# Infini-attention and GEGLU in one kernel: attention output kept transposed up to the output projection

## The chip, the cores and the metric

The kernel runs on one core of one Trainium2 chip. The metric is device time in microseconds (us) of one execution. The engines are TensorE (PE in the profile, PEld for its weight loads), VectorE (DVE), ScalarE (ACT), GpSimd (POOL) and SyncE (SP), which here issues every DMA.

## What is computed

One pre-norm transformer layer in fp32 on 2048 rows of 512. The attention has 32 heads of 16 columns and four segments of 512 rows; beside the softmax within a segment, each head reads a running memory M, z of the segments before:

```python
for s in range(N):                                   # 4 segments of L = 512 rows
    logits = einsum("bhqd,bhkd->bhqk", qs, ks) * scale + mask      # causal
    a_dot = einsum("bhqk,bhkd->bhqd", softmax(logits), vs)
    num = einsum("bhld,bhde->bhle", phi(qs), M)
    den = einsum("bhld,bhd->bhl", phi(qs), z)[..., None] + 1e-6
    outs.append(g * num / den + (1.0 - g) * a_dot)   # g = sigmoid(beta), one per head
    M = M + einsum("bhld,bhle->bhde", phi(ks), vs)
    z = z + einsum("bhld->bhd", phi(ks))
h = x + concat_heads(outs) @ wo
out = h + (gelu(n @ w_gate) * (n @ w_up)) @ w_down   # n = layernorm(h), 1376 hidden columns
```

## The kernel before, in words

**Units.** The attention works through 16 units: a chunk c of 8 heads (128 columns) in a segment s, listed in `UNITS`, segments 0 and 1 for all chunks first, then 2 and 3. A unit has two halves of four heads, numbered Q. For each unit `qkv` (L582) projects q and k (L536) and, for two chunks at once, v (L565); splits them into a high and a low part; and scatters those with DMAs into the stacked operands `stq` and `stk` (L609, L615, with a mask row L620). `pass_a` (L687) multiplies them a first time (L701) and DVE takes each row's maximum (L711), which a small transpose (L734) and a DMA (L739) put into `stq`. `pass_b` (L742) multiplies them again the other way round (L756), ScalarE takes the exponential (L760), GpSimd masks the diagonal blocks (L764), and TensorE forms P V with four heads side by side (L785, four column tiles of 32). Its result, `pv`, is transposed: for each of four heads 32 rows (16 of values, the 17th the sum of the probabilities), with the 512 queries along the columns.

**After P V.** ScalarE copies `pv` to `pvs` (L804). TensorE transposes it in four blocks (L808), so that queries stand on partitions; DVE inverts the sums (L820), multiplies them by 1 - g (L821) and scales the values (L824); GpSimd adds the memory's part (L829); a DMA stores the half's 64 columns to `o_dram` (L835).

**The memory.** `mem` (L652), for segments after the first, multiplies phi(q) as the stationary operand by the state `mb` (8 heads by 17 columns) in four matmuls (L664), two to a PSUM bank, queries again on partitions. DVE adds 1e-6, inverts, multiplies by g and scales (L671 to L681). The state is formed in `qkv`: a product (L640), masked to each head's own block on DVE (L643), added to the one before on GpSimd (L648).

**The projection.** `wo_seg` (L843) loads 128 rows of `o_dram` (L850) and of x (L851), transposes the former in four blocks (L855), splits them into high and low parts on ScalarE and DVE (L506, L507), multiplies by `wo` (L862), adds x (L866) and stores h (L868). `ln2` and the feed-forward part follow (L1031, L1092), in two passes over the halves of the rows; rows of segments 2 and 3 are read again for the second pass (L1138).

**The order.** Nothing is in program order. Each operation is given to `Sched` (L114) with an engine, an assumed duration, a priority number and the values that it reads and writes. `run` (L149) lists the operations one engine at a time: it takes the lowest priority number among those that could start within 0.059 us of the earliest. Tiles come from pools (`Pool_`, L33) when an operation is placed and return when the last user is done. The planner assumes 0.58 us for a DMA's issue and 2.2 us until it has landed. Matmuls in four column tiles are a mode of their own ("c"); a change of mode is priced at 0.1 us and held off by another 0.1. On the chip each engine and the SP queue go through their lists strictly in order and wait where an input is late.

## Time and profile before

| what | value |
|---|---|
| median of 3 runs | 850.38 us (849.77 to 851.44) |
| the profiled execution | 850.29 us |
| its span in the trace | 848.2 us |
| instructions | 15681 |
| DMA packets | 64179, 82.90 MB, mean 98 GB/s |

The page gives for each engine the time that it was busy, the chain of work that ended last (followed back from the last instruction) and the costliest groups of instructions by line. A group's row has the tile written and read, shapes, count, busy time and mean of one, and the idle time ahead of them with what ended it. A row of the timeline has the start in us from the span's start, the duration, the engine, the line and how many instructions of a kind are merged. Matmuls are pipelined, so that the durations of neighbours overlap.

### The profile page before, as it was taken

The page shows a single profiled execution, that of the slowest core. Times are in us where ns is not written, and L with a number is a line of the kernel's source. Part 1 is how long each engine was busy: PE and PEld are TensorE (multiplying, and loading weights), DVE is VectorE, ACT ScalarE, POOL GpSimd, SP SyncE. Part 2 cuts the span into 40 slices and gives each one's busy share as a digit, 9 for nine tenths or more (in the row PEclk, how much of TensorE's full clock was granted, in tenths as well). Part 3 has the DMA queues.
Part 4 walks back from the last instruction along what each step waited for, and adds up shares of the span by engine and source line. Part 5 has one row for each costly group of instructions (what it writes and reads, how often), then busy time and mean ns, then how long its engine had stood idle before and what let it go on. Part 6 is the DMA issues. An engine that isn't in the chain of part 4 may idle for free.

```text
span 848.2 us, 15681 instructions
## 1 busy us (share of the span) xinstructions
PE 825.0 (97%) x4924; PEld 656.3 (77%) x4924; DVE 621.8 (73%) x1963; ACT 511.7 (60%) x966; POOL 458.7 (54%) x791
## 2 busy tenths in 40 slices
...
GB/s 248 120 119 96 96 74 69 108 103 96 85 121 122 89 85 97 48 121 90 107 122 122 126 230 143 122 72 63 63 51 62 119 158 38 50 63 62 51 1 100
DMA packets 64179, 82.90 MB, mean 98 GB/s; under 512 B 25056, under 2 KB 27040, under 8 KB 64096
## 3 DMA queue, kind: packets, MB, share of 16 engines
...
q14 instruction: 44, 0.36, 0.2%
...
## 4 chain that ended last, share of the span: by engine, by line
PE 92%; DVE 4%; ACT 2%; issue 1%; DMA 1%; SPq 0%; POOL 0%; ACTq 0%; DVEq 0%; POOLq 0%
PE bank L1031 24%; PE bank L1092 14%; PE bank L536 10%; PE bank L701 9%; PE bank L756 9%; PE bank L785 8%; PE bank L862 5%; PE bank L565 4%; PE bank L497 2%; PE bank L808 2%; PE bank L664 1%; PE bank L640 1%; PE bank L632 1%; PE bank L855 1%; ACT pt L760 1%
## 5 line engine op out<-in xcount | busy, mean ns | idle before, releaser
L711 DVE CUSTOM_DVE_ANT_0 junk<-bank,amask 128x256 f32<-128x256 f32 (+3 forms) x512 | 231.0, 486 | 54.1 <-PE bank L701 49.8
L764 POOL TENSOR_SCALAR_AFFINE_SELECT pt<-pt 128x128 f32<-128x128 f32 (+1 forms) x448 | 131.8, 314 | 202.5 <-ACT pt L760 192.1
L760 ACT ACTIVATE pt<-bank 128x512 f32<-128x512 f32 x320 | 177.8, 602 | 63.0 <-PE bank L756 50.4
L701 PE MATMUL bank<-stk,stq 128*128 128x512 f32 (+2 forms) x384 | 130.5, 386 | 0.9 <-DVE nm L711 0.5
L756 PE MATMUL bank<-stq,stk 128*128 128x384 f32 (+3 forms) x512 | 119.8, 325 | 1.3 <-ACT pt L760 0.8
L536 PE MATMUL bank<-xt,w 128*128 128x512 f32 x384 | 109.2, 397 | 0.0
L756 PEld LDWEIGHTS bank<-stq,stk 128*128 128x128 f32 x512 | 85.8, 189 | 15.4 <-ACT pt L760 6.2
L1097 DVE TENSOR_TENSOR pt<-pt,bank 128x512 f32<-128x512 f32 x96 | 64.9, 685 | 28.7 <-PE bank L1092 28.3
L701 PEld LDWEIGHTS bank<-stk,stq 128*128 128x128 f32 x384 | 66.8, 189 | 19.5 <-issue 9.3
L536 PEld LDWEIGHTS bank<-xt,w 128*128 128x128 f32 x384 | 70.0, 189 | 10.9
L785 PE MATMUL bank<-pt,vaug 128*32 128x512 f32 (+3 forms) x1024 | 76.0, 436 | 0.0
L785 PEld LDWEIGHTS bank<-pt,vaug 128*32 128x32 f32 x1024 | 28.4, 109 | 39.9 <-issue 31.8
L1001 POOL TENSOR_TENSOR w<-raw,w 128x512 fp32r<-128x512 f32 (+2 forms) x36 | 42.4, 1180 | 25.4 <-ACT w L999 24.1
L394 POOL TENSOR_TENSOR w<-raw,w 128x512 fp32r<-128x512 f32 (+1 forms) x26 | 34.1, 1312 | 40.6 <-ACT w L389 24.0
L1031 PE MATMUL bank<-xt,stk 128*128 128x512 f32 (+1 forms) x189 | 53.0, 394 | 0.3 <-ACT pq L1038 0.3
L565 PE MATMUL bank<-wv,xt 128*128 128x256 f32 x384 | 52.7, 284 | 0.0
L565 PEld LDWEIGHTS bank<-wv,xt 128*128 128x128 f32 x384 | 50.6, 190 | 1.1
L1031 PE MATMUL bank<-xt,w 128*128 128x512 f32 (+1 forms) x183 | 50.8, 391 | 0.0
L1001 POOL TENSOR_TENSOR stk<-raw,stk 128x512 fp32r<-128x512 f32 (+3 forms) x32 | 36.9, 1155 | 20.1 <-ACT stk L999 19.7
L804 ACT ACTIVATE pvs<-bank 128x512 f32<-128x512 f32 x32 | 19.2, 598 | 44.9 <-PE bank L785 44.9
L1031 PE MATMUL bank<-stk,w 128*128 128x512 f32 (+1 forms) x162 | 45.5, 392 | 0.0
L711 DVE DVE_READ_ACCUMULATOR2_ANT nm<- 128x1 f32 x512 | 42.2, 82 | 0.0
...
## 6 DMA issues: line engine op xcount, KB each, us to landing
stq<-hl SPq DMA_DIRECT2D x96, 128.0 KB
stk<-hl SPq DMA_DIRECT2D x192, 64.0 KB
...
o_dram<-o SPq DMA_DIRECT2D x32, 128.0 KB
...
```

The source lines that it names most:

```text
L536: nc.tensor.matmul(pm.t, w.t[:, wi, dc * P:(dc + 1) * P], XT[s][dc].t[:, xi, :], start=dc == 0 and n == 0, stop=dc == ND - 1 and n == 2)
L565: nc.tensor.matmul(pm.t[:, 256 * t:256 * t + 256], XT[s][dc].t[:, xi, t0:t0 + P], whl[wi].t[:, h, 256 * (dc % 2):256 * (dc % 2) + 256], st ...
L701: nc.tensor.matmul(sa.t[:, k * w:(k + n) * w].rearrange("x (n w) -> x n w", n=n), sq.t[:, p, i * P:(i + 1) * P], sk.t[:, p, a:a + n, 0:w], ...
L711: nc.vector.tensor_tensor_reduce(out=junk.t[:, :w], in0=sa.t[:, k * w:(k + 1) * w], in1=amask[:, D - w:], op0=OP.add, op1=OP.min, scale=-1 ...
L756: nc.tensor.matmul(sc.t[:, lo:lo + D - q0], sk.t[:, p, a, q0:q0 + P], sq.t[:, p, q0:D], start=True, stop=True)
L760: act(D, prio, lambda: nc.scalar.activation(e.t, sc.t, AF.Exp), [sc], [e])
L764: nc.gpsimd.affine_select(v, v, pattern=pat + [[1, P]], compare_op=OP.is_ge, fill=0.0, base=0, channel_multiplier=-1)
L785: nc.tensor.matmul(pv.t[32 * n:32 * n + 32, kb * P:D], va.t[:, kb, 17 * j:17 * j + 32], e.t[:, lo:lo + D - kb * P], start=kb == 0, stop=la ...
L1001: pool(0.14 + 2.13e-3 * (hi - lo), prio, lambda: nc.gpsimd.tensor_tensor(v.t[:, 1, :hi - lo], r.t[:, lo:hi], v.t[:, 0, :hi - lo].bitcast(F ...
L1031: nc.tensor.matmul(dst.t[:w], v.t[:, wi, c0 + j * w:c0 + (j + 1) * w], b[bk][j].t[:, xi, :], start=first and j == 0 and n == 0, stop=j == ...
L1092: nc.tensor.matmul(pm.t, HH[p, f, s][hi].t[:w, t * P:(t + 1) * P], v.t[:w, wi, :], start=f == fl[0] and n == 0, stop=f == fl[-1] and n == 2)
L1097: dve(D, prio, lambda a=a, pm=pm: nc.vector.tensor_tensor(a.t, a.t, pm.t, op=OP.add), [pm], [a])
```

## The change

The result of P V stays transposed all the way to the output projection.

- Each half's `pvs` is stored to a DRAM scratch, `pv_dram`. After the second half, one DMA loads the unit's values as 128 rows (8 heads by 16) by 512 queries, another the 8 rows of sums as 128 partitions by 32. DVE inverts the sums and multiplies them by 1 - g; a DMA stores these factors to `r_dram`; another loads them with every head's row repeated on 16 partitions (`spread`). GpSimd multiplies, adds the memory's part in one operation for the unit, and one DMA stores the unit.
- The memory's part is made transposed as well: `mb` becomes the stationary operand of one matmul over 512 queries, and the denominators come from four matmuls in column tiles, for which the state keeps each head's z column four times (160 columns instead of 136). Their inverse goes through `r_dram` and `spread` too.
- `wo_seg` loads transposed blocks; ScalarE copies the high part from SBUF and GpSimd forms the low part.
- g is laid out by partitions, loaded by two DMAs; the row buffers fall from 6 to 4; two fills of `stk` at the start wait for the second layer norm's rows (`vcalm[1]`) instead of the first v.

```diff
-    PROW = Pool_(many("row", 6, [P, D]), fifo=True)
+    PROW = Pool_(many("row", 4, [P, D]), fifo=True)
...
+    PN = Pool_(many("n", 1, [P, D]), then=PGE)
+    PR = Pool_(many("r", 2, [P, D]), then=PGE)
+    PCD = Pool_(many("cd", 2, [P, 32]))
+    PZ = Pool_(many("z", 1, [P, P]))
...
-    PO = Pool_(many("o", 2, [P, 256]))
-    PMB = Pool_(many("mb", 7, [P, 136]))
+    PMB = Pool_(many("mb", 7, [P, 160]))
...
-    gt = sb("gt", [P, 32])
+    gt = sb("gt", [P, 2, NCH])
     tick = sb("tick", [P, 1])
-    g1 = sb("g1", [P, 32])
-    o_dram = dram.tile([T, D], F32, name="o_dram")
+    o_dram = dram.tile([NSEG, 4, P, NCH, P], F32, name="o_dram")
+    r_dram = dram.tile([16, 2, 8, D], F32, name="r_dram")
+    pv_dram = dram.tile([16, 2, P, D], F32, name="pv_dram")
...
-        if s == 0:
-            pool(0.1, prio, lambda: nc.gpsimd.tensor_copy(tick, rows[3].t[:, 0:1]), [rows[3]], [vcalm])
+        if s < 2:
+            pool(0.1, prio, lambda: nc.gpsimd.tensor_copy(tick, rows[3].t[:, 0:1]), [rows[3]],
+                 [vcalm[s]])
...
-        dve(136, prio + 0.8, lambda: nc.vector.tensor_tensor(
-            mb.t, pu.t[:, 0:136], mmask.rearrange("p j e -> p (j e)"), op=OP.mult),
-            [pu, vmmask], [mb])
+        def mask():
+            m = pu.t[:, 0:136].rearrange("p (j e) -> p j e", e=17)
+            nc.vector.tensor_tensor(mb.t[:, 0:P].rearrange("p (j e) -> p j e", e=16),
+                                    m[:, :, 0:16], mmask[:, :, 0:16], op=OP.mult)
+            nc.vector.tensor_tensor(mb.t[:, P:160].rearrange("p (j r) -> p j r", r=4),
+                                    m[:, :, 16:17].to_broadcast([P, 8, 4]),
+                                    mmask[:, :, 16:17].to_broadcast([P, 8, 4]), op=OP.mult)
+        dve(230, prio + 0.8, mask, [pu, vmmask], [mb])
         if s:
             old = MB[UNIT[c, s - 1]]
-            pool(0.44, prio + 0.8, lambda: nc.gpsimd.tensor_tensor(mb.t, mb.t, old.t, op=OP.add),
+            pool(0.49, prio + 0.8, lambda: nc.gpsimd.tensor_tensor(mb.t, mb.t, old.t, op=OP.add),
...
+        pq, mb = PQ[U], MB[UNIT[c, s - 1]]
+        pd, z, r, vr = Val(PD), Val(PZ), Val(PR), Val()
+        def den():
+            for t in range(4):
+                nc.tensor.matmul(pd.t[32 * t:32 * t + 32, 0:P], mb.t[:, P:160],
+                                 pq.t[:, t * P:(t + 1) * P], start=True, stop=True,
+                                 tile_position=(0, 32 * t), skip_group_check=True)
+        pe(0.25, prio, den, [pq, mb], [pd], acq=[z], head=0.03, tail=0.02, mode="c")
+        def inv():
+            nc.vector.tensor_scalar(pd.t[:, 0:P], pd.t[:, 0:P], 1e-6, None, op0=OP.add)
+            nc.vector.reciprocal(pd.t[:, 0:P], pd.t[:, 0:P])
+            nc.vector.tensor_scalar(z.t, pd.t[:, 0:P], gt[:, 1, c:c + 1], None, op0=OP.mult)
+        dve(1500, prio, inv, [pd, vgt], [pd, z])
+        dma(prio, lambda: nc.sync.dma_start(
+            r_dram[U, 1].rearrange("j (t q) -> t j q", t=4),
+            z.t[0:P:4]), [z], [vr])
+        spread(prio, r, U, 1, vr)
+        pm = Val(PD)
         om = OM[U] = Val(POM)
-        pq, mb = PQ[U], MB[UNIT[c, s - 1]]
-        for n in range(2):
-            pm, cc = Val(PD), Val(PCC)
-
-            def f(n=n, pm=pm):
-                for t in range(2):
-                    nc.tensor.matmul(pm.t[:, 136 * t:136 * t + 136],
-                                     pq.t[:, (2 * n + t) * P:(2 * n + t + 1) * P], mb.t,
-                                     start=True, stop=True)
-            pe(0.47, prio, f, [pq, mb], [pm], acq=[om, cc])
-
-            def nd(pm):
-                return pm.t[:, 0:272].rearrange("p (t j e) -> p t j e", t=2, j=8)
-            dve(16, prio, lambda pm=pm, cc=cc, nd=nd: nc.vector.tensor_scalar(
-                nd(pm)[:, :, :, 16], nd(pm)[:, :, :, 16], 1e-6, None, op0=OP.add), [], [pm])
-            dve(128, prio, lambda pm=pm, nd=nd: nc.vector.reciprocal(
-                nd(pm)[:, :, :, 16], nd(pm)[:, :, :, 16]), [], [pm])
-            dve(16, prio, lambda pm=pm, cc=cc, nd=nd: nc.vector.tensor_tensor(
-                cc.t, nd(pm)[:, :, :, 16],
-                gt[:, None, 8 * c:8 * c + 8].to_broadcast([P, 2, 8]), op=OP.mult), [pm, vgt], [cc])
-
-            def g(n=n, pm=pm, cc=cc, nd=nd):
-                o4 = om.t.rearrange("p (t j e) -> p t j e", t=4, j=8)
-                nc.vector.tensor_tensor(o4[:, 2 * n:2 * n + 2], nd(pm)[:, :, :, 0:16],
-                                        cc.t[:, :, :, None].to_broadcast([P, 2, 8, 16]),
-                                        op=OP.mult)
-            dve(256, prio, g, [pm, cc], [om], chain=True)
+        pe(0.87, prio, lambda: nc.tensor.matmul(pm.t, mb.t[:, 0:P], pq.t, start=True, stop=True),
+           [pq, mb, r], [pm], acq=[om])
+        dve(D, prio, lambda: nc.vector.tensor_tensor(om.t, pm.t, r.t, op=OP.mult), [pm, r], [om])
+    def spread(prio, r, U, i, vr):
+        src = r_dram[U, i]
+        dma(prio, lambda: nc.sync.dma_start(r.t, bass.AP(
+            tensor=src.tensor, offset=src.offset, ap=[[D, 8], [0, 16], [1, D]])), [vr], [r])
...
-        pvs, pn, cc, o = Val(PPVS), Val(PD), Val(PCC), Val(PO)
+        pvs = Val(PPVS)
         prio += -0.187
         act(D, prio, lambda: nc.scalar.activation(pvs.t, pv.t, AF.Copy), [pv], [pvs])
-        def tr():
-            for t in range(4):
-                nc.tensor.transpose(pn.t[:, t * P:(t + 1) * P], pvs.t[:, t * P:(t + 1) * P], ident)
-        pe(4 * TR, prio, tr, [pvs, vident], [pn], acq=[cc, o])
-        def p4():
-            return pn.t.rearrange("p (t j e) -> p t j e", t=4, j=4)
-        def c4():
-            return cc.t.rearrange("p a b -> p (a b)").rearrange("p (t j) -> p t j", t=4)
-        def o4():
-            return o.t.rearrange("p (t j e) -> p t j e", t=4, j=4)
-        j0 = 8 * c + 4 * half
-        dve(128, prio, lambda: nc.vector.reciprocal(p4()[:, :, :, 16], p4()[:, :, :, 16]), [], [pn])
-        dve(16, prio, lambda: nc.vector.tensor_tensor(
-            c4(), p4()[:, :, :, 16], g1[:, None, j0:j0 + 4].to_broadcast([P, 4, 4]),
-            op=OP.mult), [pn, vg1], [cc])
-        dve(256, prio, lambda: nc.vector.tensor_tensor(
-            o4(), p4()[:, :, :, 0:16], c4()[:, :, :, None].to_broadcast([P, 4, 4, 16]),
-            op=OP.mult), [pn, cc], [o])
+        if half == 0:
+            OUT[U] = Val()
+        dma(prio, lambda: nc.sync.dma_start(pv_dram[U, half], pvs.t), [pvs], [OUT[U]], chain=True)
+        if half == 0:
+            return
+        o, cd = Val(PN), Val(PCD)
+        src = pv_dram[U]
+        for first, ap in ((16 * D, [32, 16]), (0, [D, 16])):
+            dma(prio, lambda first=first, ap=ap: nc.sync.dma_start((cd if first else o).t, bass.AP(
+                tensor=src.tensor, offset=src.offset + first,
+                ap=[[32 * D, 8], ap, [1, ap[0]]])), [OUT[U]], [cd if first else o])
+        r, vr = Val(PR), Val()
+        def inv():
+            nc.vector.reciprocal(cd.t, cd.t)
+            nc.vector.tensor_scalar(cd.t, cd.t, gt[:, 0, c:c + 1], None, op0=OP.mult)
+        dve(500, prio, inv, [cd, vgt], [cd])
+        dma(prio, lambda: nc.sync.dma_start(
+            r_dram[U, 0].rearrange("j (b q) -> (j b) q", q=32), cd.t), [cd], [vr])
+        spread(prio, r, U, 0, vr)
+        pool(1.24, prio, lambda: nc.gpsimd.tensor_tensor(o.t, o.t, r.t, op=OP.mult), [r], [o])
         if s:
-            om = OM[U]
-            pool(0.69, prio, lambda: nc.gpsimd.tensor_tensor(
-                o4(), o4(), om.t.rearrange("p (t j e) -> p t j e", t=4, j=8)[
-                    :, :, 4 * half:4 * half + 4, :], op=OP.add), [om], [o])
-        def st():
-            dst = o_dram[s * D:(s + 1) * D, c * P + 64 * half:c * P + 64 * half + 64]
-            nc.sync.dma_start(dst.rearrange("(t p) e -> p t e", p=P),
-                              o.t.rearrange("p (t e) -> p t e", t=4))
-        dma(prio, st, [o], [OD[s]], chain=True)
+            pool(1.24, prio, lambda: nc.gpsimd.tensor_tensor(o.t, o.t, OM[U].t, op=OP.add),
+                 [OM[U]], [o])
+        dma(prio, lambda: nc.sync.dma_start(
+            o_dram[s, :, :, c].rearrange("t p q -> p t q"),
+            o.t.rearrange("p (t q) -> p t q", t=4)), [o], [OD[s]], chain=True)
...
-            ro, rx, ot, pt, pm = Val(PROW), Val(PROW), Val(POT), Val(PD), Val(PD)
+            ro, rx, ot, pm = Val(PROW), Val(PROW), Val(POT), Val(PD)
             rows.append(rx)
-            dma(prio, lambda ro=ro, r0=r0: nc.sync.dma_start(ro.t, o_dram[r0:r0 + P]), [OD[s]], [ro])
+            dma(prio, lambda ro=ro, t=t: nc.sync.dma_start(
+                ro.t, o_dram[s, t].rearrange("p c q -> p (c q)")), [OD[s]], [ro])
             dma(prio, lambda rx=rx, r0=r0: nc.sync.dma_start(rx.t, x[r0:r0 + P]), [OD[s]], [rx])
-            def tr(ro=ro, pt=pt):
-                for dc in range(ND):
-                    nc.tensor.transpose(pt.t[:, dc * P:(dc + 1) * P],
-                                        ro.t[:, dc * P:(dc + 1) * P], ident)
-            pe(4 * TR, prio, tr, [ro, vident], [pt], acq=[ot])
-            split_psum(prio, pt, ot)
+            act(D, prio, lambda ro=ro, ot=ot: nc.scalar.activation(ot.t[:, 0], ro.t, AF.Copy), [ro],
+                [ot], src=0.092)
+            pool(1.23, prio, lambda ro=ro, ot=ot: nc.gpsimd.tensor_tensor(
+                ot.t[:, 1], ro.t, ot.t[:, 0].bitcast(F32), op=OP.subtract), [ro], [ot])
...
-    dma(1, lambda: nc.sync.dma_start(
-        gt, bass.AP(tensor=beta.tensor, offset=beta.offset, ap=[[0, P], [1, 32]])), XT[1], [vgt])
-    act(32, 1, lambda: nc.scalar.activation(gt, gt, AF.Exp, scale=-1.0), [vgt], [vgt])
+    pool(0.1, 0.5, lambda: nc.gpsimd.memset(gt, 0.0), [], [vgt])
+    for i, ap in enumerate([[[NCH, 8], [0, 16], [1, NCH]], [[0, 4], [NCH, 8], [1, NCH]]]):
+        dma(1, lambda i=i, ap=ap: nc.sync.dma_start(
+            gt[0:P:4 if i else 1, i], bass.AP(tensor=beta.tensor, offset=beta.offset, ap=ap)), XT[1], [vgt],
+            chain=True)
+    act(8, 1, lambda: nc.scalar.activation(gt, gt, AF.Exp, scale=-1.0), [vgt], [vgt])
     def c_gate():
         nc.vector.tensor_scalar(gt, gt, 1.0, None, op0=OP.add)
         nc.vector.reciprocal(gt, gt)
-        nc.vector.tensor_scalar(g1, gt, -1.0, 1.0, op0=OP.mult, op1=OP.add)
-    dve(600, 1, c_gate, [vgt], [vgt, vg1])
+        nc.vector.tensor_scalar(gt[:, 0], gt[:, 0], -1.0, 1.0, op0=OP.mult, op1=OP.add)
+    dve(500, 1, c_gate, [vgt], [vgt])
...
-            c_stk(2, [VA[0]])
-            c_stk(3, [VA[0]])
+            c_stk(2, [vcalm[1]])
+            c_stk(3, [vcalm[1]])
```

20 lines of the change are left out of this document (10 added, 10 removed).

## The prediction

> **What bounds the kernel now.** I read the page first: the busy line, then the chain that ended last. After them come the table by stages (us, then each engine's busy time and count, TensorE's granted clock, the DMA share, GB/s) and the list of waits.
>
> ```profile
> PE 825.0 (97%) x4924; PEld 656.3 (77%) x4924; DVE 621.8 (73%) x1963; ACT 511.7 (60%) x966; POOL 458.7 (54%) x791
> PE 92%; DVE 4%; ACT 2%; issue 1%; DMA 1%; SPq 0%; POOL 0%; ACTq 0%; DVEq 0%; POOLq 0%
> ```
> ```profile
> 0.00:50.00 50.00, 36.83 (x214) 31.86 (x215) 37.85 (x111) 36.58 (x71) 26.02 (x46) 0.97 0.59 178
> 100.00:150.00 50.00, 50.00 (x382) 37.47 (x382) 38.25 (x165) 32.66 (x63) 20.43 (x61) 1.00 0.34 78
> 450.00:500.00 50.00, 47.13 (x299) 34.46 (x300) 39.09 (x114) 30.41 (x57) 28.62 (x54) 1.00 0.45 148
> ```
>
> TensorE is the bound: 825.0 of 848.2 us, 92% of the chain, and a stage like 100 to 150 without any idle time. Its clock is 1.00 there, so only less work on it, or less waiting, shortens the kernel. Of the 23 us of idle time, 13.2 lie in the first 50 us, where weights and rows arrive and which the change hardly touches, and 2.9 in the stage 450 to 500. Elsewhere a us taken from TensorE is a us of the kernel, and a us that it waits anew is one lost. The profiled execution took 850.29 us, 2.1 more than its span; the median of the three runs is 850.38, so no correction is made between them.
>
> **The change part by part: TensorE.** Matmuls overlap, so a duration overstates what one costs. I take the distance from one start to the next start on the engine instead.
>
> ```profile
> L808 PE MATMUL bank<-ident,pvs x128: 270/272/327, 68.9 to 488.6; 128*128 128x128 f32 x128
> L855 PE MATMUL bank<-ident,row x64: 270/272/275, 397.7 to 542.5; 128*128 128x128 f32 x64
> L664 PE MATMUL bank<-mb,pq x96: 277/279/371, 48.6 to 434.5; 128*128 128x136 f32 x96
> ```
> ```profile
> 150.86 0.60 PE L808 MATMUL bank<-ident,pvs 128*128 128x128 f32 x4
> 151.22 0.71 PE L701 MATMUL bank<-stk,stq 128*128 128x512 f32 x2
> ...
> 160.41 0.68 PE L701 MATMUL bank<-stk,stq 128*128 128x512 f32 x2
> 160.93 0.62 PE L664 MATMUL bank<-mb,pq 128*128 128x136 f32 x4
> 161.30 0.77 PE L756 MATMUL bank<-stq,stk 128*128 128x384 f32 x4
> ...
> 164.40 1.71 PE L785 MATMUL bank<-pt,vaug 128*32 128x512 f32 x16
> 166.04 0.73 PE L701 MATMUL bank<-stk,stq 128*128 128x512 f32 x2
> 166.71 0.86 PE L785 MATMUL bank<-pt,vaug 128*32 128x128 f32 x16
> 167.49 0.50 PE L701 MATMUL bank<-stk,stq 128*128 128x256 f32 x2
> ```
> ```profile
> 492.95 0.60 PE L855 MATMUL bank<-ident,row 128*128 128x128 f32 x4
> 493.30 0.95 PE L1031 MATMUL bank<-stk,w 128*128 128x512 f32 x3
> ```
>
> Removed:
> - The transposes after P V (L808): 128, in 32 groups of four. One group is 150.86 to 151.22, 0.36 us: 11.5 us.
> - The transposes ahead of the output projection (L855): 16 groups, 492.95 to 493.30, 0.35 us: 5.6 us.
> - The memory product (L664): 96 records, four to a group of two matmuls (each leaves two records), so 24 groups at 160.93 to 161.30, 0.37 us: 8.9 us.
>
> Together 26.0 us. Added are 12 products of 512 columns and 12 denominators, four matmuls of 32 rows side by side over 128 columns. No row shows either form. Nearest are the four-abreast matmuls of L785, also plain fp32. The first excursion into them passes 512+384 columns in 1.64 us (164.40 to 166.04), the second 128+256 in 0.78 (166.71 to 167.49). So 512 columns cost 0.86 us, 1.68 ns each, and 0.135 us per excursion is fixed. On leaving, the pair at 166.04 takes 0.67 us where the pair at 160.41 took 0.52: 0.15 more. One excursion costs about 0.3 us.
>
> - Product: 512 columns by 1.68 ns, 0.86 us, 12 times: 10.3 us. From L664's 272 columns in 0.37 us it would be 0.70 each, 8.4; from 896 columns in 1.64 us, 0.94, 11.3. I take the middle, which has the fixed part taken out.
> - Denominator: 128 columns by 1.68 ns, 0.215 us: 2.6 us.
> - Excursions: in the changed program's order on TensorE, 11 of the 12 denominators stand right beside a P V group and share its excursion; counted over the program there are 39 excursions instead of 34. 5 by 0.3 us: 1.5 us, and at most 12 by 0.3, 3.6.
>
> Together 14.4 us (12.5 to 17.5). [...] Balance on TensorE: -26.0 + 14.4 = -11.6 us (-8.5 to -13.5).
>
> One wait goes with the transposes: at 488 TensorE stands still for a PSUM bank that a late addition holds.
>
> ```profile
> 488.23 0.63 PE L808 MATMUL bank<-ident,pvs 128*128 128x128 f32 x4 [2.10 <-DVE row L866]
> ```
>
> The last transposes after P V were queued ahead of feed-forward matmuls that were ready (L1031 follows at once). In the changed order those stand there themselves. I take -2.1 us, at worst 0.
>
> **DVE, ScalarE, GpSimd.** These cost nothing unless they make TensorE wait.
>
> ```profile
> L824 DVE TENSOR_TENSOR o<-bank,cc 128x256 f32<-128x256 f32 x32 | 13.5, 420 | 0.5
> L820 DVE RECIPROCAL bank<-bank 128x16 f32<-128x16 f32 x32 | 8.5, 264 | 3.9 <-PE bank L808 3.3
> L681 DVE TENSOR_TENSOR om<-bank,cc 128x256 f32<-128x256 f32 x24 | 10.0, 420 | 0.3
> L673 DVE RECIPROCAL bank<-bank 128x16 f32<-128x16 f32 x24 | 5.9, 255 | 0.1
> L507 DVE TENSOR_TENSOR wv<-bank,wv 128x512 fp32r<-128x512 f32 x16 | 10.9, 684 | 3.1 <-ACT wv L506 3.1
> L643 DVE TENSOR_TENSOR mb<-bank,mmask 128x136 f32<-128x136 f32 x12 | 3.5, 296 | 1.9 <-PE bank L640 1.7
> L829 POOL TENSOR_TENSOR o<-o,om 128x256 f32<-128x256 f32 x24 | 17.8, 741 | 23.9 <-DVE o L824 22.4 <-DVE mm L727 0.7 <-DVE ln L466 0.6
> L394 POOL TENSOR_TENSOR w<-raw,w 128x512 fp32r<-128x512 f32 x25 | 32.8, 1313 | 40.6 <-ACT w L389 24.0 <-PE bank L1031 14.9 <-PE bank L701 1.3
> ```
> ```profile
> L951 DVE RECIPROCAL gt<-gt x1: 353/353/353, 39.3 to 39.3; 128x32 f32<-128x32 f32 x1
> ```
>
> DVE loses 13.5+8.5+10.0+5.9+10.9 = 48.8 us in these rows. It gains 12 inversions of 128x128: a reciprocal of 32 columns took 0.353 us, of 16 0.264, so 5.6 ns a column, 0.89 us for 128, and two operations near L643's 0.30, 1.5 us: 18 us. It also gains 16 small inversions of about 0.5 us (8 us) and 12 products of about 0.69 (8 us), some 34 in all: relief. ScalarE copies the projection's input from SBUF instead of PSUM, the same count. GpSimd loses 17.8 us and gains 12+16 operations of 512 columns and 16 low halves of the projection's input, 44 by 1.31: 58 us, so +40 on an engine that was 41% busy in the stage 100 to 150. Price for TensorE here: nothing, while masks run ahead; the cover is weighed as a rival. The projection's single split buffer now waits for GpSimd's 1.31 us instead of DVE's 0.68 between two tiles; feed-forward and attention matmuls stand between (uncovered, 16 by 0.63, 10 us). The 12 products on TensorE wait for no DMA in the changed order; their multiplication on DVE waits for the spread factor, with pass_a's maxima behind it.
>
> **SyncE and the round trips.** 32 stores of L835 go; 32 stores, 32 loads, 16+12 factor stores and 16+12 spreads come, and 16 stores: 136 for 32, 104 more, about 6.5 a unit on one queue in order.
>
> ```profile
> stq<-hl SPq DMA_DIRECT2D x96, 128.0 KB
> stk<-hl SPq DMA_DIRECT2D x192, 64.0 KB
> ```
> ```profile
> 288.99 4.67 SPq L615 DMA_DIRECT2D stk<-hl  x6
> 293.70 0.55 SPq L620 DMA_DIRECT2D stq<-amask  x1
> ```
> ```profile
> 295.54 0.68 PE L701 MATMUL bank<-stk,stq 128*128 128x512 f32 x2
> ```
> ```profile
> 494.50 0.37 SPq L835 DMA_DIRECT2D o_dram<-o  x1
> 497.97 0.32 SPq L850 DMA_DIRECT2D row<-o_dram  x1
> ```
> ```profile
> 500.92 0.60 PE L855 MATMUL bank<-ident,row 128*128 128x128 f32 x4
> ```
>
> A store to DRAM and the load of what it wrote stood 3.5 us apart (494.50 to 497.97, the queue waiting); the load's reader began 2.95 us after (500.92). A round is about 6.4 us at most, and a unit now has two, with an inversion between: 13 to 14 us, against 27 us per unit (16 units in about 430 us, from L664's and L808's first starts to their last). The memory factor needs one round; in the changed order 44 or more DVE instructions stand between its inversion and its product, by the page's mean (621.8/1963 = 0.32 us) 14 us: covered. After the last unit the chain delays segments 2 and 3 only, which the second feed-forward pass reads far later.
>
> Priced at nothing, too: the projection's row buffers fall from six to four, so a row's load can wait for an earlier row, with attention or feed-forward matmuls beside it (uncovered, 2.95 us a segment, 12 us); two fills at the start wait for another value, and beta comes in two loads, before anything reads them.
>
> [...]
>
> What the queue delays for others is another thing. A store or factor that waits blocks what stands behind it: the stk and stq loads, whose reader is pass_a on TensorE. Six stk loads were issued until 293.66, and TensorE's first matmul on them started at 295.54, 1.9 us later: little reserve there. An extra 6.5 issues take 2.4 (at 0.37) to 3.6 us (at 0.55). Lower bound of the price: 0, for the added issues fall into the queue's waiting time. Upper: 16 units by 2.5 us, 40 us. I take 2 us in all, near the lower end, because the row of the tightest unit shows TensorE arriving after the load and not waiting for it, and both ends stay in the rivals.
>
> Sum: -11.6 - 2.1 + 2.0 = -11.7 us; 850.3 - 11.7 = 838.6, say **838.5 us**.
>
> **The rivals.**
> A. *The SyncE queue comes to set the time (slower).* Place: stk/stq loads and row maxima standing behind a store or spread that waits for another DMA's landing. Price: the unit's 2.5 us of added issue plus one uncovered landing (3.5 less those 2.5, 1.0), less the 1.9 us reserve, 1.6 us of TensorE waiting each: 16 by 1.6 = 26 us, instead of 2. Time 838.5 - 2 + 26 = 862; with half of the units, 849.5. It decides from 13.7/16 = 0.86 us of waiting per unit. For it: 1.9 us of reserve. Against it: the 288 stq and stk loads take 4.67/6 = 0.78 us each, 225 of the 430 us, so the queue has room for 104 issues more.
> B. *GpSimd's masks come late.* Its multiplications wait for a spread and take 1.3 us each, ahead of masks that P V needs.
>
> ```profile
> PEld bank L785 <- POOL pt L764: 7.4, 27, 0.4
> ```
>
> P V's weight loads already wait for masks 27 times, so half of the 28 operations exposed cost 14 by 0.65 us, 9 us: 847.5.
> C. *The new products cost TensorE more.* At 17.5 us and with the stall of 488 only moved: 838.5 + 3.1 + 2.1 = 843.7.
> D. *The queued work is reordered for the better*, with DVE's relief shortening waits within the attention: 834.
>
> **How the numbers follow.** Forecast 0.57 (835 to 842), D 0.05, C 0.08, B 0.10 (843 to 853), A 0.20 (mostly 852 to 862). The range takes in all but the upper part of A and the far end of D: 833 to 856. This kernel can be told from no change at about 0.2%, 1.7 us. Faster: 0.57 + 0.05 + 0.08 + half of B, 0.75. Within 0.2%: 0.04 of B. Slower: A and the rest of B, 0.21.
>
> **What would show it.** Right: no transposes behind P V or ahead of the projection, TensorE's busy time near 813 us at a share of 97%, 12 products at 0.86 us start to start, stages from 100 to 450 still at 49.5 or more of 50. Wrong by A: idle time ahead of pass_a's weight loads ended by DMA landings, and SyncE waits on the new stores. Wrong by B: more idle time ahead of P V ended by GpSimd. Wrong by C: products over 0.94 us, or excursions above 39.

## The result, and the profile after

The changed kernel is slower: a median of 865.41 us (862.38 to 866.66, four runs) against 850.46 us (849.77 to 851.44), a ratio of 1.0166 [1.0143, 1.0190], 15 us. The forecast was 838.5 us, and the time lies 9 us above the upper end of the range. The profiled execution took 862.38 us, with a span of 860.7. Two medians further down, of e2 and e16, leave out one far longer execution each (1567 and 4544 us); with it they would be 852.23 and 874.88 us.

Read the page of the changed kernel first, the busy line and the chain that ended last:

```profile
span 860.7 us, 15357 instructions
PE 824.5 (96%) x4756; PEld 636.2 (74%) x4756; DVE 615.1 (71%) x1847; ACT 513.6 (60%) x966; POOL 493.7 (57%) x813
PE 67%; DVE 10%; DMA 7%; POOL 5%; SPq 4%; issue 4%; ACT 2%; POOLq 0%; ACTq 0%; DVEq 0%
```

TensorE still bounds the kernel, but only 67% of the chain is its own work, where it was 92%; DVE, DMAs, GpSimd and the SyncE queue have 26%. Its idle time is 860.7 - 824.5 = 36.2 us, 13.0 more than before (848.2 - 825.0 = 23.2). Its busy time fell by 0.5 us where I forecast 11.6. The span grew by 13.0 - 0.5 = 12.5 us. So two things want a cause: the new idle time, and the busy time that did not fall.

Two stages of the changed kernel (length in us, then the busy time and count of PE, PEld, DVE, ACT and POOL, the granted clock, the DMA share, GB/s):

```profile
100.00:150.00 50.00, 46.88 (x324) 36.41 (x326) 35.51 (x152) 28.87 (x57) 20.79 (x60) 0.97 0.42 114
...
450.00:500.00 50.00, 47.43 (x272) 31.17 (x269) 35.01 (x115) 30.65 (x57) 29.12 (x55) 0.97 0.55 174
```

The stage 100 to 150, which had no idle microsecond, now has 3.1, and its clock has fallen to 0.97. DVE, ScalarE and TensorE are all less busy there than before: nobody is the bound, and all of them wait.

Who waits for whom stands in the list of waits (total us, times, longest):

```profile
POOL n L840 <- DMA r<-r_dram: 32.1, 10, 7.2
...
PEld bank L715 <- DVE nm L725: 17.0, 42, 2.7
PEld bank L799 <- POOL pt L778: 16.1, 37, 1.3
POOL n L840 <- issue: 10.8, 3, 6.5
...
DVE cd L834 <- DMA cd<-pv_dram: 6.6, 7, 2.8
```

L799 is P V (L785 before) and L778 its mask (L764). P V's weight loads waited 7.4 us for masks before and wait 16.1 now. GpSimd itself waits: L840, the multiplication of a unit's values by the spread factors, stood still for 32.1 us until the spread had landed, and for 10.8 more that the profile names issue. Those are the spread too: at these three places it began 0.1 to 0.2 us after a spread's landing (113.53 and 113.66, 167.59 and 167.71, 478.07 and 478.20), and the values had landed at least 4.8 us earlier, as at every one of the 16 places. So GpSimd stood for the spread for 42.9 us.

One unit shows the chain of DMAs. The timeline of the changed kernel from 326 us on (start, duration, engine, line, and in brackets the idle time ahead):

```profile
326.66 0.63 SPq L828 DMA_DIRECT2D cd<-pv_dram  x1
...
329.45 0.33 SPq L837 DMA_DIRECT2D r_dram<-cd  x1
...
333.22 0.63 SPq L697 DMA_DIRECT2D r<-r_dram  x1
...
337.36 1.26 POOL L840 TENSOR_TENSOR n<-n,r 128x512 f32<-128x512 f32 x1 [7.21 <-DMA r<-r_dram]
```

The sums are asked for at 326.66, inverted on DVE at 328.80, their factors stored at 329.45. The spread is issued at 333.22, and GpSimd can multiply at 337.36, 4.1 us later. GpSimd had finished its last mask at 330.14 and stood for 7.2 us. Here this cost TensorE nothing: ScalarE began the next exponentials only at 339.12, so no mask was being kept back.

Another unit shows what it costs where masks are due:

```profile
313.62 1.27 POOL L840 TENSOR_TENSOR n<-n,r 128x512 f32<-128x512 f32 x1 [3.21 <-DMA r<-r_dram]
...
314.84 0.29 POOL L778 TENSOR_SCALAR_AFFINE_SELECT pt<-pt 128x128 f32<-128x128 f32 x1
315.11 1.29 POOL L842 TENSOR_TENSOR n<-n,om 128x512 f32<-128x512 f32 x1
...
316.35 2.29 POOL L778 TENSOR_SCALAR_AFFINE_SELECT pt<-pt 128x128 f32<-128x128 f32 x9
...
318.62 1.27 POOL L397 TENSOR_TENSOR w<-raw,w 128x512 fp32r<-128x512 f32 x1
...
319.83 0.77 POOL L778 TENSOR_SCALAR_AFFINE_SELECT pt<-pt 128x256 f32<-128x256 f32 x2
...
320.30 0.99 PE L799 MATMUL bank<-pt,vaug 128*32 128x256 f32 x8 [0.80 <-POOL pt L778]
```

GpSimd stood for 3.2 us for the spread, while ScalarE finished four exponentials between 310.93 and 313.55. It takes its list in order, so their masks came after the multiplication, and it worked from 313.62 on without a pause. P V's weight loads from 317.06 to 320.66 waited 2.3 us for masks, and TensorE stood quite idle for 0.80 of them. One more operation stood in front of the last masks: L397, a split of the feed-forward weights.

The planner had assumed 0.58 + 2.2 = 2.8 us for each DMA from issue to landing. Worked out from the trace's semaphore events (from a DMA's issue to the last of the events that it left), the 28 spreads took 4.2 us (median; one in ten over 5.5) and the 16 loads of the values (`n<-pv_dram`) 4.5. The small loads of the sums took 2.1. Before, most DMAs landed in 1.9 to 2.9 us.

**The busy time that did not fall.** The groups of P V's matmuls, first in the kernel before, then in the changed one:

```profile
L785 PE MATMUL bank<-pt,vaug 128*32 128x512 f32 (+3 forms) x1024 | 76.0, 436 | 0.0
```
```profile
L799 PE MATMUL bank<-pt,vaug 128*32 128x512 f32 (+3 forms) x1024 | 84.2, 443 | 3.8 <-POOL pt L778 3.8
```

The same 1024 matmuls are busy for 8.2 us more. Four of them run side by side, and while one of the four waits for its mask the others still count as busy, so that part of a wait hides in the busy time. One group shows it:

```profile
283.08 3.05 PE L799 MATMUL bank<-pt,vaug 128*32 128x512 f32 x32
```

Its 32 matmuls take 3.05 us without a pause and at a granted clock of 1.00; a like group at 83.10 (its row stands further down) takes 2.36 us. Within it the weight loads waited 0.70 us for masks. The other part is the clock. After this pause TensorE is granted half of it for a while:

```profile
130.69 0.35 DVE L834 RECIPROCAL cd<-cd 128x32 f32<-128x32 f32 x1 [2.81 <-DMA cd<-pv_dram]
...
132.55 0.79 PE L715 MATMUL bank<-stk,stq 128*128 128x512 f32 x1 [2.50 <-DVE nm L725]
```
```profile
131.50:132.50 1.00, 0.00 (x0) 0.00 (x0) 1.00 (x6) 0.00 (x0) 0.00 (x0) 0.88 0.63 203
132.50:136.00 3.50, 3.45 (x12) 3.06 (x12) 1.87 (x6) 0.62 (x2) 0.54 (x2) 0.55 0.19 64
```

A pause of 2.50 us ends at 132.55. DVE, whose maxima TensorE lacked, had itself stood for 2.81 us until the sums had landed (L834): this pause is the rival's of the next section, not GpSimd's. After it the granted clock of the next 3.5 us is 0.55 on average. The trace has four such dips of 3.4 us at 0.5 (from about 132, 443, 487 and 695 us on); the kernel before had one, at 29. The mean clock of the changed kernel is 0.991, against 0.998 before: by estimate 0.009 x 860.7 = 7.7 us lost against 0.002 x 848.2 = 1.7. Which pauses bring a dip is not shown: the kernel before stood for 2.10 us ahead of 488.23, and its clock stayed at 1.00 (486 to 491).

### The profile page after: what moved, and what is told of

It is laid out like the page before. It is cut to its first block, busy times and chain, and to the rows that moved or that the text cites. A ratio compares the mean times of both kernels' runs of the same rounds, so it can differ in the third digit from the quotient of the medians.

```text
span 860.7 us, 15357 instructions
## 1 busy us (share of the span) xinstructions
PE 824.5 (96%) x4756; PEld 636.2 (74%) x4756; DVE 615.1 (71%) x1847; ACT 513.6 (60%) x966; POOL 493.7 (57%) x813
## 2 busy tenths in 40 slices
DMA packets 71261, 103.51 MB, mean 120 GB/s; under 512 B 13836, under 2 KB 24396, under 8 KB 71180
## 4 chain that ended last, share of the span: by engine, by line
PE 67%; DVE 10%; DMA 7%; POOL 5%; SPq 4%; issue 4%; ACT 2%; POOLq 0%; ACTq 0%; DVEq 0%
PE bank L1043 20%; PE bank L1104 13%; PE bank L715 6%; PE bank L540 6%; PE bank L770 6%; PE bank L799 6%; PE bank L871 4%; DVE junk L725 3%; SPq L619 2%; PE bank L569 2%; DMA r<-r_dram 2%; PE bank L500 1%; POOL pt L778 1%; DMA cd<-pv_dram 1%; PE bank L690 1%
## 5 line engine op out<-in xcount | busy, mean ns | idle before, releaser
L778 POOL TENSOR_SCALAR_AFFINE_SELECT pt<-pt 128x128 f32<-128x128 f32 (+1 forms) x448 | 129.9, 312 | 164.2 <-ACT pt L774 158.0
L799 PE MATMUL bank<-pt,vaug 128*32 128x512 f32 (+3 forms) x1024 | 84.2, 443 | 3.8 <-POOL pt L778 3.8
L540 PEld LDWEIGHTS bank<-xt,w 128*128 128x128 f32 x384 | 70.6, 191 | 11.5 <-DVE xt L510 0.2
L799 PEld LDWEIGHTS bank<-pt,vaug 128*32 128x32 f32 x1024 | 29.9, 110 | 47.5 <-issue 29.7
L397 POOL TENSOR_TENSOR w<-raw,w 128x512 fp32r<-128x512 f32 (+1 forms) x26 | 33.5, 1289 | 35.5 <-ACT w L392 35.3
L1043 PE MATMUL bank<-xt,w 128*128 128x512 f32 (+1 forms) x168 | 47.2, 399 | 0.0
L840 POOL TENSOR_TENSOR n<-n,r 128x512 f32<-128x512 f32 x16 | 20.6, 1286 | 44.5 <-DMA r<-r_dram 32.1
L1013 POOL TENSOR_TENSOR w<-raw,w 128x512 fp32r<-128x512 f32 (+2 forms) x33 | 38.1, 1155 | 12.9 <-ACT w L1011 12.9
L1043 PE MATMUL bank<-stk,w 128*128 128x512 f32 (+1 forms) x135 | 38.1, 390 | 0.0
L1020 POOL TENSOR_TENSOR raw<-raw,raw 128x256 f32<-128x256 f32 (+1 forms) x44 | 35.7, 811 | 3.1
```

The costliest lines, as they stand in the source:

```text
L540: nc.tensor.matmul(pm.t, w.t[:, wi, dc * P:(dc + 1) * P], XT[s][dc].t[:, xi, :], start=dc == 0 and n == 0, stop=dc == ND - 1 and n == 2)
L778: nc.gpsimd.affine_select(v, v, pattern=pat + [[1, P]], compare_op=OP.is_ge, fill=0.0, base=0, channel_multiplier=-1)
L799: nc.tensor.matmul(pv.t[32 * n:32 * n + 32, kb * P:D], va.t[:, kb, 17 * j:17 * j + 32], e.t[:, lo:lo + D - kb * P], start=kb == 0, stop=la ...
L1013: pool(0.14 + 2.13e-3 * (hi - lo), prio, lambda: nc.gpsimd.tensor_tensor(v.t[:, 1, :hi - lo], r.t[:, lo:hi], v.t[:, 0, :hi - lo].bitcast(F ...
L1043: nc.tensor.matmul(dst.t[:w], v.t[:, wi, c0 + j * w:c0 + (j + 1) * w], b[bk][j].t[:, xi, :], start=first and j == 0 and n == 0, stop=j == ...
```

## The experiments

**Theory.** GpSimd, held by the spread, is late with the masks; P V waits, and with it TensorE. **Rivals:** DVE, held by the load of the sums, is late with pass_a's maxima; the SyncE queue is too full; four row buffers are too few; the order of the queues, which the planner makes anew for every program, has got worse by itself.

### The wait taken away, the order kept

In the next three kernels each engine's list is that of the changed kernel, apart from the exchanged operands and one constant that is filled at the start.

`e9_pool_no_spread`: GpSimd multiplies the values by themselves instead of by the spread factors, so it waits for no spread. All DMAs remain. The scaling of the softmax part is left out.

```diff
-        pool(1.24, prio, lambda: nc.gpsimd.tensor_tensor(o.t, o.t, r.t, op=OP.mult), [r], [o])
+        pool(1.24, prio, lambda: nc.gpsimd.tensor_tensor(o.t, o.t, o.t, op=OP.mult), [r], [o])
```

> The changed kernel in the same order on every engine, with all its DMAs; only GpSimd multiplies the P V values by themselves, so it no longer waits for the spread (it leaves out the scaling by the inverted sums). Theory G (GpSimd standing at its multiplication until the spread lands holds back masks and so P V): 855 to 859 instead of 865.4. Theory D (DVE standing at its inversion until the sums land holds back maxima): 863 to 867.

Measured: 853.54 us, 1.0034 [1.0024, 1.0044] of the kernel before. Against the changed kernel's 1.0166 that is 1.3%, 11 us. Its waits:

```profile
PEld bank L715 <- DVE nm L725: 15.3, 42, 1.6
...
PEld bank L799 <- POOL pt L778: 7.5, 20, 1.4
...
POOL n L840 <- DMA n<-pv_dram: 2.7, 2, 2.1
```

The time lies below theory G's range, so the wait was worth more than expected. GpSimd's wait is 2.7 us instead of 42.9, and P V's wait for masks is back at 7.5, where it was 7.4 before. P V's busy time is 79.6 us. The clock did not recover (0.989), so the gain is not the clock. So three quarters of the loss of 15 us, 11 to 12 us, come from this one wait. By which way it reaches TensorE is not separated: through the masks, or also through the stores of a unit's result (L844), for which the SyncE queue waited on GpSimd for 48.6 us in the changed kernel and 16.3 here. (The multiplication is also a little shorter, 1.04 us instead of 1.29, 4 us of GpSimd's time in 16.)

`e10_dve_no_sums`: DVE inverts a tile of ones instead of the loaded sums, so it waits for no load; everything else stays. The division by the sums is left out.

```diff
-            dma(prio, lambda first=first, ap=ap: nc.sync.dma_start((cd if first else o).t, bass.AP(
+            dma(prio, lambda first=first, ap=ap: nc.sync.dma_start(cdl[U % 2] if first else o.t, bass.AP(
...
-            nc.vector.reciprocal(cd.t, cd.t)
+            nc.vector.reciprocal(cd.t, cdc)
```

> The same order and DMAs again; DVE inverts a constant tile, so it no longer waits for the load of the sums (the true sums are loaded into another tile and left out). Theory D: 854 to 860. Theory G: 863 to 867.

Measured: 863.84 us, 1.0149 [1.0121, 1.0177]. This is theory G's range, and the interval holds the changed kernel's 1.0166; a cost of some us isn't excluded. TensorE's side shows a trade: pass_a's weight loads waited 13.1 us for maxima instead of 17.0, and P V's 20.4 for masks instead of 16.1.

`e11_neither` makes both edits.

> Both of the edits above. If G and D are the whole of the attention's added waiting (some 14 us with the clock's dips after TensorE's pauses): 848 to 853. If SyncE's lateness itself (maxima and stk landing late) holds most: 858 to 864.

Measured: 853.10 us, 1.0030 [1.0012, 1.0048], the time of e9, at the upper end of the first range. The two waits do not add up. The spread's is the one that counts.

### The spread landing sooner, the order kept

`e1_wide`: the spread and the load of the values walk 16 outer rows instead of 8. The loads carry the same bytes; a chunk's columns are laid out with the value's index outside and the head's inside, and the rows of `wo` are permuted to match.

```diff
-            tensor=src.tensor, offset=src.offset, ap=[[D, 8], [0, 16], [1, D]])), [vr], [r])
+            tensor=src.tensor, offset=src.offset, ap=[[0, 16], [D, 8], [1, D]])), [vr], [r])
...
-        for first, ap in ((16 * D, [32, 16]), (0, [D, 16])):
+        for first, ap in ((16 * D, [[32 * D, 8], [32, 16], [1, 32]]), (0, [[D, 16], [32 * D, 8], [1, D]])):
```

> Same order of instructions on every engine as the changed kernel (865.4 us); only the address order of two kinds of loads changes: the spread and the load of the P V values now walk 16 outer rows of 8 instead of 8 outer rows of 16 (each chunk's columns are kept in that order, and the rows of wo with them). In the changed kernel the spread lands 4.1 us and the value load 4.5 us after issue, where ordinary loads of the same size took 2.6 to 2.9. Theory L (these two loads land late, and GpSimd and DVE stand waiting for them ahead of masks and maxima): both land in about 2.8 us and the time falls to 850 to 857. Theory Q (the SyncE queue issues everything too late, since its planned issue times are too short): landing may fall, the time stays at 860 to 866. Theory P (the new products and mode changes cost TensorE more): stays at 865.

Measured: 855.65 us, 1.0050 [1.0034, 1.0066]: 10 us less than the changed kernel. By the same semaphore events the spread now lands in 3.6 us instead of 4.2, the load of the values in 3.6 instead of 4.5. The events differ in number too: the changed kernel's spread issued at 333.22 raised its semaphore in nine steps (the first 1.05 us after the issue, the other eight from 3.62 to 4.06), e1's at 327.74 in sixteen (3.15 to 3.66), and so did all 28 spreads and 16 loads of values in each. e1 has 14188 packets of under 512 bytes against 13836, 352 more, which is 8 for each of the 44. Why 16 outer rows land sooner is not shown.

```profile
POOL n L839 <- DMA r<-r_dram: 17.6, 7, 4.9
POOL n L839 <- issue: 9.6, 3, 6.3
POOL n L839 <- DMA pv_dram<-pvs: 6.3, 1, 6.3
```

L839 is the changed kernel's L840. These three add up to 33.5 us, against 42.9 in the changed kernel. The time is in theory L's range, though the landings are not its 2.8 us. Landings that come 0.6 and 0.9 us sooner are worth 10 us here. GpSimd's list was held by the spread: in the changed kernel the values had landed 4.8 us or more ahead of the multiplication at every place.

### The planner told how long the DMAs take

`e2_told`: the planner is given durations nearer to the measured ones. The instructions are the same; their order is not.

```diff
-                            [hl] + first, [dst], chain=True)
+                            [hl] + first, [dst], dur=0.78, chain=True)
...
-            tensor=src.tensor, offset=src.offset, ap=[[D, 8], [0, 16], [1, D]])), [vr], [r])
+            tensor=src.tensor, offset=src.offset, ap=[[D, 8], [0, 16], [1, D]])), [vr], [r], lat=3.6)
...
-        dma(prio, lambda: nc.sync.dma_start(pv_dram[U, half], pvs.t), [pvs], [OUT[U]], chain=True)
+        dma(prio, lambda: nc.sync.dma_start(pv_dram[U, half], pvs.t), [pvs], [OUT[U]], lat=2.8, chain=True)
...
-                ap=[[32 * D, 8], ap, [1, ap[0]]])), [OUT[U]], [cd if first else o])
+                ap=[[32 * D, 8], ap, [1, ap[0]]])), [OUT[U]], [cd if first else o], lat=2.2 if first else 4.0)
```

> Same instructions and DMAs as the changed kernel; the planner is given the durations that its trace showed: 3.6 us until a spread has landed, 4.0 for the value load, 2.8 for the P V store (it assumed 2.2), and 0.78 us for each stq/stk issue (it assumed 0.58). Theory L and theory Q both expect less waiting: 845 to 856. Theory P: 863 to 867, since TensorE's work is the same.

Measured: 851.74 us, 1.0007 [0.9993, 1.0022], as expected. Some 13 us come back by four other numbers in the planner and the order that it draws from them; which of the four counts was not separated. GpSimd's idle time ahead of L840 falls to 21.9 us.

`e3_wide_queue`: e1 with the planner told only the 0.78 us that the issue of an stq or stk load takes.

> The wide loads of the first run, and the planner told of the 0.78 us issue alone. If L and Q each hold a part, this is the fastest of the three: 840 to 850. If Q alone matters it equals the second run; if L alone matters it equals the first.

Measured: 851.71 us, 1.0004 [0.9992, 1.0016], 4 us less than e1 but not the fastest of the three: it equals e2. By what was expected, the issue's time alone is then worth as much as all of e2's numbers; each is also another order.

`e4_no_pv_factor`: the load of the sums, their inversion, the store and the spread are left out; GpSimd multiplies the values by themselves. The values are thus not scaled. The order is planned anew.

```diff
-        o, cd = Val(PN), Val(PCD)
+        o = Val(PN)
...
-        pool(1.24, prio, lambda: nc.gpsimd.tensor_tensor(o.t, o.t, r.t, op=OP.mult), [r], [o])
+        pool(1.24, prio, lambda: nc.gpsimd.tensor_tensor(o.t, o.t, o.t, op=OP.mult), [], [o])
```

> Leaves out the division of P V by its sums: no load of the sums, no inversion, no factor store, no spread; GpSimd multiplies the values with themselves instead, so its work is the same. 48 DMAs and 32 DVE operations fewer; the value load and the memory's factor stay. Theory L or Q: most of the waiting goes with this chain, 842 to 852. Theory P: 860 to 865. If it stays near 865 the memory's chain or the value load is to blame.

Measured: 865.09 us, 1.0160 [1.0138, 1.0182]: nothing gained, though less is done, and a miss: 842 to 852 was expected if the chain after P V held the waiting. The multiplication's group (L830 here) points to the reason:

```profile
L830 POOL TENSOR_TENSOR n<-n 128x512 f32<-128x512 f32 x16 | 16.7, 1042 | 60.1 <-DMA n<-pv_dram 50.8 <-PE bank L715 6.1 <-DMA stk<-hl 3.3
```

The planner, free of the spread, put the multiplication right behind the load of the values, of which it believed 2.8 us and which lands after 4.6. GpSimd's wait didn't go, it moved to another slow load and grew. A kernel that is planned anew doesn't take a single wait away.

### Row buffers

`e5_before_rows4`: the kernel before with four row buffers.

```diff
-    PROW = Pool_(many("row", 6, [P, D]), fifo=True)
+    PROW = Pool_(many("row", 4, [P, D]), fifo=True)
```

> The kernel before (851 us) with four row buffers instead of six, nothing else. Theory R (the fewer row buffers delay the projection, whose matmuls should fill TensorE while the last units of attention wait for ScalarE): 856 to 866, the loss between 380 and 500 us. Theory W (the loss in that stage comes from the longer chain after P V or from GpSimd, not from the buffers): 850 to 853.

Measured: 862.57 us, 1.0144 [1.0123, 1.0165], 11 to 12 us more. It is theory R's time, but not its place, 380 to 500 us. One place can be seen. The stage 680 to 700 of the kernel before, and of e5, with e5's waits there:

```profile
680.00:700.00 20.00, 20.00 (x90) 16.44 (x89) 17.44 (x29) 11.93 (x24) 13.02 (x15) 1.00 0.52 155
```
```profile
680.00:700.00 20.00, 16.71 (x74) 13.19 (x73) 17.19 (x36) 13.53 (x24) 11.05 (x12) 0.91 0.62 191
```
```profile
PEld bank L497 <- DVE vaug L891: 2.0, 1, 2.0
PEld bank L1031 <- POOL xt L902: 1.9, 1, 1.9
```

The rows of the second feed-forward pass are read again, normalised and transposed (L497). With six buffers the last of them were normalised from 666 to 668 us and transposed from 669 on; with four they were normalised from 684 to 687, and TensorE is idle for 3.3 us at a lower clock. The changed kernel shows the same pause at 692 (1.7 us ahead of L500, 1.5 ahead of L1043). That it needs four buffers is not shown: kernels with six in another order also idle between 640 and 720 us (e13 2.2 us, e14 3.0, the kernel before 0.5, e5 3.4), and e2 and e3, with four, have no half clock there. In all, e5 is idle for 5.6 us more than the kernel before and busy for 5.5 us more; the latter is not explained. In the stage 450 to 500 it is idle for only 1.7 us more.

`e6_after_rows6` is the changed kernel with six row buffers.

> The changed kernel (865.4 us) with six row buffers again, nothing else. Theory R: 852 to 860, the waiting of the attention itself stays and that between 380 and 500 us falls to what it was before. Theory W: 862 to 868.

Measured: 874.11 us, 1.0267 [1.0250, 1.0284], 9 us more than with four: a miss, above both ranges. Two more buffers in a list scheduler mean another order everywhere, and this one was worse.

`e7_told_rows6` is e2 with six row buffers.

> The second run's kernel (planner told the durations, 852.2 us) with six row buffers. Its attention was already 8.7 us ahead of the kernel before at the 17th P V and lost that lead after 380 us. Theory R: the lead is kept, 836 to 844. Theory W: 850 to 854.

Measured: 845.68 us, 0.9936 [0.9921, 0.9951], between the two ranges, 6 us less than e2 and faster than the kernel before. e5, e6 and e7 together do not tell the price of the row buffers: by e5 four cost 12 us, by e6 they save 9, by e7 they cost 6, and each step draws another order too.

`e8_told_rows6_dve` is e7 with the low half of the projection's input formed on DVE again instead of GpSimd (in `wo_seg`).

```diff
-            pool(1.23, prio, lambda ro=ro, ot=ot: nc.gpsimd.tensor_tensor(
+            dve(D, prio, lambda ro=ro, ot=ot: nc.vector.tensor_tensor(
```

> As the run just before, and the low half of the projection's input is formed on DVE again instead of GpSimd (0.68 instead of 1.29 us, and GpSimd is left to masks). If the single split buffer or GpSimd's load holds the projection back: 3 to 8 us below the run just before. If not: within 2 us of it.

Measured: 855.12 us, 1.0040 [1.0025, 1.0056]: 9 us more than e7, outside both expectations. Nothing here speaks for a loss by the split on GpSimd; how much of the 9 us is order stays open.

### Everything mended

`e12_told_rows6_wide` puts together the planner's numbers of e2, six row buffers and the 16 outer rows of e1.

> The kernel with planner told and six row buffers (845.7 us) with the wide loads of the first run, in its order, so that loads land earlier than the planner now believes. If late landings still cost something there: 840 to 844. If they are covered: 844 to 847.

Measured: 843.87 us, 0.9916 [0.9899, 0.9932], the fastest kernel of this study, 6.5 us below the 850.35 of the kernel before beside it. Its interval overlaps that of e7, so what the 16 outer rows add once the planner knows the times is not shown. Its page, its waits and its P V group:

```profile
PE 813.5 (97%) x4756; PEld 633.8 (75%) x4756; DVE 616.1 (73%) x1847; ACT 509.3 (60%) x966; POOL 495.5 (59%) x813
PE 82%; DVE 6%; ACT 4%; POOL 4%; issue 3%; DMA 1%; SPq 0%; ACTq 0%; DVEq 0%; POOLq 0%
```
```profile
PEld bank L715 <- DVE nm L725: 13.8, 40, 1.0
...
PEld bank L799 <- POOL pt L778: 5.2, 19, 0.4
POOL n L840 <- DMA r<-r_dram: 1.9, 3, 1.2
```
```profile
L799 PE MATMUL bank<-pt,vaug 128*32 128x512 f32 (+3 forms) x1024 | 76.6, 436 | 0.0
```

TensorE's busy time is 813.5 us, the 813 of the forecast; P V is back at 76.6, and GpSimd waits 1.9 us for spreads. A large part of what is still missing to 838.5 us lies where attention hands over to the feed-forward part:

```profile
460.00:470.00 10.00, 7.98 (x35) 5.57 (x28) 8.10 (x11) 5.66 (x11) 6.22 (x12) 0.69 0.42 131
470.00:480.00 10.00, 7.40 (x48) 4.72 (x46) 8.69 (x15) 9.08 (x18) 10.00 (x13) 0.79 0.40 131
```

Here 2.0 + 2.6 us are idle, and the clock gives 0.69 and 0.79 of its rate, by estimate 5 us more. In the kernel before, the whole stage from 450 to 500 had 2.9 us of idle time at a clock of 1.00. Between 60 and 380 us e12 is idle for 3.2 us against 1.7 before, between 640 and 720 for 2.9 against 0.5.

### How much is order

In the last six kernels only `window` in `Sched.run` (0.059 us) differs: the instructions are the same, in another order. Two such orders were made of the kernel before, of the changed one and of e12.

```diff
-    def run(self, window=0.059, stay=0.1):
+    def run(self, window=0.05, stay=0.1):
```

> The kernel before, with the planner's window at 0.05 us in place of 0.059: the same instructions, durations, buffers and DMAs, queued in another order from the first attention units on. If an order is worth only a few us (theory: the change's cost lies in the late spread and the row buffers, and the order follows), 848 to 853 us. If the order by itself moves the time as much as the change did (rival: the change merely lost the order that the kernel before had), 855 to 865.

> As the kernel with 0.05, with 0.07 us. Theory: 848 to 853 us. Rival, that the kernel before had an exceptional order: 855 to 865.

> The changed kernel with the planner's window at 0.05 us: same instructions, another order. Theory, that the late spread and the four row buffers cost the time in any order: 859 to 868 us. Rival, that the changed kernel met a bad order: 845 to 857.

> As the kernel with 0.05, with 0.07 us. Theory: 859 to 868 us. Rival, a bad order: 845 to 857.

> The kernel with the truer planner's numbers, six row buffers and 16-row spreads, window at 0.05 us. Theory, that its gain comes from less work on TensorE with the waits mended: 841 to 848 us, still below the kernel before. Rival, that it met a lucky order: 850 to 860.

> As the kernel with 0.05, with 0.07 us. Theory: 841 to 848 us. Rival, a lucky order: 850 to 860.

| window | kernel before | changed | e12 | changed less before | e12 less before |
|---|---|---|---|---|---|
| 0.059 | 850.46 | 865.41 | 843.87 | +15.0 | -6.6 |
| 0.05 | 856.76 (1.0059 [1.0042, 1.0076]) | 874.64 (1.0271 [1.0254, 1.0288]) | 850.16 (0.9993 [0.9980, 1.0006]) | +17.9 | -6.6 |
| 0.07 | 855.62 (1.0051 [1.0036, 1.0066]) | 873.86 (1.0261 [1.0230, 1.0292]) | 846.05 (0.9939 [0.9916, 0.9962]) | +18.2 | -9.6 |

All ratios are against the kernel before as it stands. The theory's ranges were missed on the high side by e13, e14, e15, e16 and e17; only e18 lies within. The times of e13, e14 and e17 are the rival's, those of e15 and e16 lie above both ranges. So the rival holds in part: the kernel before did meet a good order, 5 to 6 us better than its two others. An order alone is worth 2 to 9 us, more than expected, and of the three windows 0.059 was the best for each kernel. As the whole explanation the rival falls: the change costs 15 to 18 us in each of the three windows, its three times (865 to 874) lie clear of those before (850 to 857), and the mended version gains 6 to 10 against the kernel before of the same window. The means of three are 854.3, 871.3 and 846.7 us. The waits of GpSimd are large in e15 and e16:

```profile
POOL n L840 <- DMA r<-r_dram: 60.8, 13, 7.3
```
```profile
POOL n L840 <- DMA r<-r_dram: 25.7, 8, 6.5
POOL n L840 <- issue: 24.7, 6, 8.3
```

In e17 they are 9.1 us, in e18 5.7 and 14.6 more named issue. So kernel by kernel they are larger in the changed one, but within one kernel the larger wait is not always the longer time: e18 waits for 20 us and takes 846, e17 for 9 and takes 850. Where an order differs, a time must be compared over several orders. This bears on e5 too: against the two other orders with six buffers (855.6 and 856.8), its 862.6 us are only 6 to 7 more, and only one order with four buffers was run, so the price of the row buffers stays open.

## Why the prediction was wrong, point by point

- **TensorE's work: the product's price was right, the balance partly by luck.** The product's price was 0.86 us. In the changed kernel it stands between its neighbours like this:

```profile
98.06 0.63 PE L770 MATMUL bank<-stq,stk 128*128 128x512 f32 x2
98.53 0.34 PE L715 MATMUL bank<-stk,stq 128*128 128x384 f32 x1
98.71 1.02 PE L690 MATMUL bank<-pq,mb 128*128 128x512 f32 x2
99.16 1.04 PE L715 MATMUL bank<-stk,stq 128*128 128x512 f32 x2
100.03 0.62 PE L770 MATMUL bank<-stq,stk 128*128 128x512 f32 x2
```

  The next start comes 0.45 us after the product's, but the two matmuls that follow then take until 100.03: 1.32 us for the product and a pair that takes 0.47 elsewhere (98.06 to 98.53), so 0.85. A start alone would have misled. The denominators, forecast at 2.6 us and 1.5 for excursions:

```profile
83.10 2.36 PE L799 MATMUL bank<-pt,vaug 128*32 128x512 f32 x32
85.27 0.40 PE L674 MATMUL bank<-pq,mb 128*32 128x128 f32 x8
85.61 0.62 PE L715 MATMUL bank<-stk,stq 128*128 128x384 f32 x2
```

  One takes 0.34 us, 12 of them 4.1, the sum of the two terms. There are 39 excursions in the trace, as forecast. The balance of -11.6 us agrees with e12's busy time, 813.5 - 825.0 = -11.5, but the clock had a part in it: e12 was busy for 9.7 us at half clock and the kernel before for 3.05, so that at an equal clock the work fell by an estimated 15 us, more than the stated -8.5 to -13.5. Rival C, dearer products, falls.
- **DVE, ScalarE, GpSimd "cost nothing unless they make TensorE wait": this step failed.** GpSimd's added 40 us of work stood in the sum as "Price for TensorE here: nothing, while masks run ahead", and masks did not always run ahead. Rival B had 9 us for it, as half of the 28 operations at 0.65 us. What counted was not the multiplication but the wait in front of it on a queue in order: 42.9 us at 13 of 16 places. It cost TensorE 11 to 12 us by e9. B had the right place, masks behind a GpSimd that waits for a spread, but its price was that of the work and not of the wait; that 9 came near 11 is luck, and its time of 847.5 us was not reached. Of the 27 us between 838.5 and the measured 865.4, e9 accounts for 11 to 12. The 15 that remain in e9 (853.5) no run takes apart: TensorE is idle there for 32.2 us where the forecast's terms leave 23.1 (23.2 - 2.1 + 2.0) and busy for 819.6 us where they give 813.4, with 17 us at half clock, by estimate 8.5 us lost.
- **The round trips: mis-sized.** A landing was taken as 2.95 us, from loads of `o_dram` and its readers. The spread took 4.2 and the values' load 4.5. The forecast set 13 to 14 us for a unit's two rounds against 27 us per unit and found them covered. The unit had the time; the planner, which believed 2.8 us, had not left it, and put the multiplication where it thought the spread had landed. For a chain through DRAM the cover is what the order has left between issue and reader, and each of the 16 had to be looked at in the changed order.
- **The row buffers, priced at nothing, with 12 us if uncovered: open.** e5 with four is 6 to 12 us longer than three orders with six, and idle for 3.3 us at the second pass's rows, which the forecast did not look at: it thought of the projection's rows alone. But e6 went the other way by 9 us, and order alone is worth as much. The projection's split on GpSimd, also at nothing, showed no loss (e8).
- **SyncE, +2.0 us, and rival A: not seen as a wait of TensorE.** One half of A's sign is there, the SyncE queue waiting for the new stores (48.6 us for GpSimd at L844). The other half is not: TensorE waited for landed stk loads next to never:

```profile
L715 PE MATMUL bank<-stk,stq 128*128 128x512 f32 (+2 forms) x384 | 130.0, 391 | 5.0 <-DVE nm L725 4.3 <-DMA stk<-hl 0.3
```

  Row maxima (`stq<-mx`) held pass_b's weight loads for 2.5 us. Rival A's 862 us came near the measured time by another way. A time that fits is no proof of a mechanism.
- **The stall at 488, -2.1 us: replaced.** The stage 450 to 500 has 2.6 us of idle time instead of 2.9, with the clock at 0.97.
- **Not thought of:** that the clock can fall as well where TensorE pauses (four dips to 0.5 instead of one, by estimate 6 us), and that a change to a list-scheduled kernel also draws another order, worth up to 9 us.

Two things stay open. pass_a's weight loads wait for DVE's maxima much longer than before (17.0 us against 2.4; still 13.8 in e12). In e10, without the wait for the sums, 13.1 us of it stay, so that wait is some 4 us of it; the inversions on DVE stand ahead of the maxima (0.97 us each for 128 columns, L681), but no kernel without them was run. And why the handover at 460 to 480 stays slow in e12 isn't settled; its order is another one there, too.
